# Chunked decay attention and experts on one core: state products in four quarters of the array, state update behind the values, a third first-layer accumulator

## The chip, the cores and the metric

One core of one Trainium2 chip runs the whole program. The metric is device time in microseconds: three runs of the kernel before gave 942.53, 943.29 and 944.0, median 943.29.

## The reference

A decay attention over 4 batches, 8 heads, 768 positions and 48 dimensions per head feeds four experts, each with two layers and a ReLU between them.

```python
for t in range(S):
    cur = einsum('bhd,bhe->bhde', u * k[t], v[t])
    y[:, :, t] = einsum('bhd,bhde->bhe', r[t], state + cur)
    state = w[t][..., None] * state + einsum('bhd,bhe->bhde', k[t], v[t])
x = y.transpose(0, 2, 1, 3).reshape(B * S, H * D)          # 3072 x 384
for e in range(4):
    out += p[:, e:e+1] * (relu(x @ w1[e]) @ w2[e])         # 384 -> 1024 -> 384
```

## The kernel before, in words

The 768 positions are cut into 6 chunks of 128. A chunk of one batch is a **unit**: 24 units, four to a chunk, units 0 to 3 in chunk 0. The 8 heads form 4 pairs. Of a pair i, head j=0 lies on partitions 0 to 47 and head j=1 on 64 to 111 (`half(j)`), so that its products use one half of the rows of the TensorE array; the results of j=0 and j=1 go to the lower and the upper half of the PSUM partitions (`wide(j)`).

A unit goes through six steps, handed out one at a time by `go()`:
- `step_a`: decays of the next unit (DVE), then `scores`: eight products of k and r into two PSUM banks (`sc`, L235), and four transposes of k (`kt`, L241), which ScalarE copies to `ks`.
- `step_b`: the second scan (`e`, L216) and, from chunk 1 on, the decayed state `sd`.
- `step_c`: `masking`, two predicated copies of the scores into `a` (L251).
- `step_d`: scaling of the next unit's r and k, and its diagonal.
- `step_e`: `values`. From chunk 1 on, eight **state products** (`yp`, L261, 48 rows by 48 or 64 columns), then eight **value products** (L266, 128 rows), all in one bank. ScalarE copies the result to `y3` and `x`, VectorE writes the rests that the copies lose (L273 to L276), and `fill` moves the fourth pair by two DMAs into the rows of `x` that are left free.
- `step_f`: `carry`, the **state update**: eight products of 48 moving columns (`up`, L295), which VectorE adds to the state (L300); in chunk 0 ScalarE copies them (L298).

The experts' work is the frame. A turn is one expert on one chunk: eight first-layer tiles of nine products (`f1`, L332; ScalarE writes `hh` at L338 and VectorE `hl` at L339, and only then is the accumulator `pf1` free), then for each batch 24 second-layer products (`f2`, L352). After each f1 tile, and eight times in the second half of a turn, there is a gap; `gap()` adds `pace` to a credit and hands out one step for each whole credit. Chunk 0's first turn is cut into two segments of two batches (256 columns in place of 512), and the second segment needs the x of units 2 and 3. All engines work strictly in the written order. PSUM's eight banks are: two f1 accumulators, two for f2, two for scores (one buffer), two for `kt`, `yp` and `up` in turn.

Of the kernel before, what the change touches and what calls it, by code (L numbers as in the profile page):

```python
# [8 lines left out]
F32 = mybir.dt.float32  # L9
# [11 lines left out]
C = 128  # L21
# [23 lines left out]
def chunked_path(ctx, tc, dmaj, tmaj, u_bc, probs, w1, w2, out, flag):  # L45
    nc = tc.nc

    def pool(name, bufs, space=None):
        kw = {} if space is None else {"space": space}
        return ctx.enter_context(tc.tile_pool(name=name, bufs=bufs, **kw))  # L50
# [7 lines left out]
    p_in = pool("in", 2)  # L58
    p_one = pool("one", 1)
    p_two = pool("two", 2)  # L60
    ps_f1 = pool("ps_f1", 2, PS)
    ps_f2 = pool("ps_f2", 2, PS)
    ps_sc = pool("ps_sc", 1, PS)
    ps_mi = pool("ps_mi", 2, PS)


    ident = const.tile([128, 128], F32, name="ident")
# [161 lines left out]
    def scores(n):  # L229

        s = un[n]
        sc = [ps_sc.tile([128, NP, C], F32, name=f"sc{j}", tag=f"sc{j}") for j in range(2)]
        for i in range(NP):
            for j in range(2):
                nc.tensor.matmul(sc[j][:, i, :], s["kk"][half(j), i, :], s["rr"][half(j), i, :],  # L235
                                 start=True, stop=True)
        last = s["c"] == NCH - 1
        if not last:
            kt = ps_mi.tile([128, NP, 128], F32, name="kt", tag="mi")
            for i in range(NP):  # L240
                nc.tensor.transpose(kt[:, i, 0:ROWS], s["kk"][:, i, :], ident[0:ROWS, 0:ROWS])  # L241
        s["sc"] = sc
        if not last:
            ks = p_one.tile([128, NP, ROWS], F32, name="ks", tag="ks")
            nc.scalar.copy(ks, kt[:, :, 0:ROWS])
            s["ks"] = ks

    def masking(n):
        s = un[n]
        for j in range(2):  # L250
            nc.vector.copy_predicated(s["a"][j], mask.unsqueeze(1).to_broadcast([128, NP, C]), s["sc"][j])  # L251

    def values(n):
        s = un[n]
        c, b, v = s["c"], s["b"], s["v"]
        y = ps_mi.tile([128, NP, C], F32, name="yp", tag="mi")

        if c > 0:
            for i in range(NP):
                for j in range(2):  # L260
                    nc.tensor.matmul(y[wide(j), i, :], sd[n % 2][half(j), i * D:i * D + (64 if j == 0 else D)],  # L261
                                     s["rr"][half(j), i, :], start=(i == 0), stop=False, skip_group_check=True)
        for i in range(NP):
            for j in range(2):
                h = 2 * i + j
                nc.tensor.matmul(y[wide(j), i, :], v[:, h * D:h * D + (64 if j == 0 else D)], s["a"][j][:, i, :],  # L266
                                 start=(c == 0 and i == 0), stop=(i == NP - 1), skip_group_check=True)
        if c not in xb:
            xb[c] = p_x.tile([128, KT, B, 2, C], F32R, name="x", tag="x")
        x = xb[c]  # L270
        y3 = s["y3"] = p_two.tile([ROWS, 2, C], F32R, name="y3", tag="y3")

        nc.scalar.copy(y3[:, 0], y[0:ROWS, KT, :])  # L273
        nc.scalar.copy(x[0:ROWS, :, b, 0, :], y[0:ROWS, 0:KT, :])
        nc.vector.tensor_tensor(y3[:, 1], y[0:ROWS, KT, :], y3[:, 0].bitcast(F32), ALU.subtract)
        nc.vector.tensor_tensor(x[0:ROWS, :, b, 1, :], y[0:ROWS, 0:KT, :], x[0:ROWS, :, b, 0, :].bitcast(F32),  # L276
                                ALU.subtract)

    def fill(n):

        s = un[n]
        for j in range(2):
            nc.sync.dma_start(out=xb[s["c"]][64 * j + D:64 * (j + 1), :, s["b"]].bitcast(F32),
                              in_=s["y3"][half(j)].bitcast(F32))

    def carry(n):
        s = un[n]
        c, b, v = s["c"], s["b"], s["v"]
        if c == NCH - 1:
            return  # L290
        up = ps_mi.tile([128, NP, D], F32, name="up", tag="mi")
        for i in range(NP):
            for j in range(2):
                h = 2 * i + j
                nc.tensor.matmul(up[wide(j), i, :], s["ks"][:, i, wide(j)], v[:, h * D:(h + 1) * D],  # L295
                                 start=True, stop=True)
        if c == 0:
            nc.scalar.copy(st[b], up[0:ROWS])  # L298
        else:
            nc.vector.tensor_tensor(st[b], sd[n % 2][:, 0:NP * D].rearrange("p (i e) -> p i e", i=NP), up[0:ROWS],  # L300
                                    ALU.add)
# [93 lines left out]

    def step_e(n):
        values(n)
        load(n + 2, "r")
        fill(n)
        if n + 1 < NU:  # L400
            guard(n + 1)
        load(n + 3, "w")

    def step_f(n):
        carry(n)
        load(n + 2, "v")
        if n == NU - 1:
            un[n]["big"] = verdict()
        else:
            del un[n]  # L410

    def step_g(n):
        flag_it(un.pop(n)["big"])

    parts = (step_a, step_b, step_c, step_d, step_e, step_f)
    steps = [(f, n) for n in range(NU) for f in parts]
    steps += [(None, NU - 1)] * 8 + [(step_g, NU - 1)]
    steps.reverse()
    read = set()

# [57 lines left out]
    with tc.manual_schedule():  # L478
        act_table()
        setup_a()  # L480
        for what in ("w", "k", "r", "own"):
            load(0, what)
        nc.sync.dma_start(out=u_sb, in_=u_bc)
        load(0, "v")
        warm_up(FILL[0])
        for what in ("w", "k", "r", "own", "v"):
            load(1, what)
        nc.sync.dma_start(out=pr, in_=probs)
        for q in range(NQ):
# [12 lines left out]
        load(2, "own")  # L502
        guard(0)
        load(2, "w")
        own_product(1)
        until_decays(1)
        scale(1)
        warm_up(FILL[1])
        values(0)
        fill(0)  # L510
        own_score(1)
        carry(0)
        load(2, "v")
        scores(1)
        split_w((0, 1, 0), True)
        masking(1)
        after_decays(2)
        own_product(2)
        warm_up(FILL[2])
        values(1)  # L520
        fill(1)
        split_w((0, 1, 1), True)
        guard(1)
        setup_c()
        until_decays(2)
        split_w((0, 1, 2), True)
        carry(1)
        for what in ("w", "k", "r", "v"):
            load(3, what)
        for q in range(3):  # L530
            more_raw()
        scale(2)
        own_score(2)
        load(3, "own")
        split_w((0, 1, 3), True)
        owed.append(None)
        guard(2)
        load(4, "w")
        warm_up(FILL[3])
        del un[0], un[1], steps[-2 * len(parts):]  # L540
        for pi, (g, e) in enumerate(passes):
            first, last = pi % NE == 0, pi % NE == NE - 1
            for blk in g:
                segs = SEG if pi == 0 else (B,)
                b0 = 0
                for nb in segs:
                    next_w1 = blk == g[-1] and pi + 1 in fresh and b0 + nb == B
                    own_w2 = blk == g[0] and pi in fresh and b0 == 0
                    if pi == 0:
                        pace[:] = (0.75, 0.75) if b0 == 0 else (0.25, 0.5)  # L550
                    elif blk >= GROUPS[-1][0]:
                        pace[:] = 0.75, 1.25
                    else:
                        pace[:] = 0.5, 1.0

                    def work(i):
                        q = i % FT // 2
                        if own_w2 and i < FT and i % 2 == 0:
                            split_next((e, 2, q), pi > 0 or q != 1)
                        if next_w1 and i >= FT and i % 2 == 0:  # L560
                            split_next((passes[pi + 1][1], 1, q), True)
                        if i == FT - 1 and last and b0 + nb == B:
                            read.add(blk)

# [193 lines left out]
```

## Time and profile before

| | |
|---|---|
| median of three runs | 943.29 us |
| profiled execution | 942.36 us, span 940.6 us |
| TensorE products busy (PE) | 915.4 us, 97% |
| TensorE weight loads busy (PEld) | 817.9 us, 87% |
| VectorE, ScalarE, GpSimd | 356.2, 254.3, 278.2 us |
| mean granted TensorE clock | 0.985 |

One product in full fp32 shows as two matmul records (x16 for eight products); the fp32r products of the experts show as one. A record's own duration holds the latency of the array, so the time that a group takes is read from the start of the group to the start of the next.

### The profile page before, as it was taken

The page shows a single profiled execution, that of the slowest core. Times are in us where ns is not written, and L with a number is a line of the kernel's source. Part 1 is how long each engine was busy: PE and PEld are TensorE (multiplying, and loading weights), DVE is VectorE, ACT ScalarE, POOL GpSimd, SP SyncE. Part 2 cuts the span into 40 slices and gives each one's busy share as a digit, 9 for nine tenths or more (in the row PEclk, how much of TensorE's full clock was granted, in tenths as well). Part 3 has the DMA queues.
Part 4 walks back from the last instruction along what each step waited for, and adds up shares of the span by engine and source line. Part 5 has one row for each costly group of instructions (what it writes and reads, how often), then busy time and mean ns, then how long its engine had stood idle before and what let it go on. Part 6 is the DMA issues. An engine that isn't in the chain of part 4 may idle for free.

```text
span 940.6 us, 13680 instructions
## 1 busy us (share of the span) xinstructions
PE 915.4 (97%) x5617; PEld 817.9 (87%) x5617; DVE 356.2 (38%) x567; ACT 254.3 (27%) x462; POOL 278.2 (30%) x283
## 2 busy tenths in 40 slices
PE   7589999999999999999999999999999999999997
PEld 5589888898989899889888898998998899899887
DVE  7744545554444532221355553112212212222221
ACT  3434434322224312312321223133103301321210
POOL 4745757431406613304312230024003200131000
PEclk8789999999999999999999999999999999999999
DMA  8544444332215312202322320012001200020001
GB/s 246 179 127 134 132 156 144 120 101 76 87 36 180 107 54 68 68 1 68 102 84 79 100 73 6 22 51 85 1 1 45 74 17 1 1 67 28 16 26 38
DMA packets 34536, 70.49 MB, mean 75 GB/s; under 512 B 4512, under 2 KB 13088, under 8 KB 34464
## 3 DMA queue, kind: packets, MB, share of 16 engines
q1 hardware_dynamic: 34464, 69.52, 23.6%
q8 instruction: 46, 0.75, 0.3%
q14 instruction: 26, 0.21, 0.1%
HBM read 62.43 MB, written 4.72 MB: 71 GB/s over the span
## 4 chain that ended last, share of the span: by engine, by line
PE 95%; DMA 2%; DVE 1%; ACT 1%; issue 0%; SPq 0%
PE pf L352 43%; PE pf L332 42%; PE yp L266 3%; PE sc L235 3%; PE yp L261 2%; PE up L295 1%; PE kt L241 1%; DMA k<-in_dmaj 1%; DMA raw<-in_w 1%; DMA wx<-in_dmaj 0%; DVE w2l L142 0%; DMA x<-y 0%; DVE k L227 0%; ACT w1h L137 0%; ACT wx L307 0%
## 5 line engine op out<-in xcount | busy, mean ns | idle before, releaser
L332 PE MATMUL pf<-x,w1h 128*128 128x512 f32 (+1 forms) x1200 | 364.7, 386 | 12.0 <-DMA x<-y 6.4
L332 PEld LDWEIGHTS pf<-x,w1h 128*128 128x128 f32 x1200 | 223.9, 191 | 55.9 <-issue 7.5
L352 PE MATMUL pf<-w2h,hh 128*128 128x384 f32 x768 | 261.2, 340 | 0.0
L352 PE MATMUL pf<-w2h,hl 128*128 128x384 f32 x768 | 257.1, 335 | 0.0
L352 PE MATMUL pf<-w2l,hh 128*128 128x384 f32 x768 | 256.9, 334 | 0.0
L339 DVE SCALAR_TENSOR_TENSOR hl<-pf,hh 128x512 fp32r<-128x512 f32 (+1 forms) x200 | 133.8, 669 | 280.4 <-ACT hh L338 279.7
L338 ACT ACTIVATE hh<-pf 128x512 fp32r<-128x512 f32 (+1 forms) x200 | 116.2, 581 | 451.1 <-PE pf L332 451.0
L332 PE MATMUL pf<-x,w1l 128*128 128x512 f32 (+1 forms) x600 | 230.5, 384 | 0.0
L142 POOL TENSOR_TENSOR w1l<-raw,w1h 128x384 fp32r<-128x384 f32 x80 | 84.4, 1084 | 255.0 <-ACT w1h L137 254.6
L352 PEld LDWEIGHTS pf<-w2h,hh 128*128 128x128 f32 x768 | 144.2, 188 | 4.8 <-issue 3.3
L352 PEld LDWEIGHTS pf<-w2l,hh 128*128 128x128 f32 x768 | 144.3, 188 | 0.7
L352 PEld LDWEIGHTS pf<-w2h,hl 128*128 128x128 f32 x768 | 144.1, 188 | 0.0
L332 PEld LDWEIGHTS pf<-x,w1l 128*128 128x128 f32 x600 | 114.7, 191 | 21.8
L361 DVE SCALAR_TENSOR_TENSOR acc<-pf,pr,acc 128x384 f32<-128x384 f32 x72 | 44.5, 618 | 201.0 <-PE pf L352 201.0
L142 POOL TENSOR_TENSOR w2l<-raw,w2h 128x384 fp32r<-128x384 f32 x78 | 79.0, 1034 | 115.9 <-ACT w2h L137 110.8
L192 POOL TENSOR_TENSOR a<-ident,dg 128x512 f32<-128x512 f32 x45 | 46.7, 1057 | 133.7 <-DVE dg L184 105.6
L235 PEld LDWEIGHTS sc<-r,k 48*128 48x128 f32 x384 | 24.7, 197 | 12.1 <-DVE k L227 6.1
L235 PE MATMUL sc<-r,k 48*128 48x128 f32 x384 | 29.5, 296 | 5.3 <-DVE k L227 5.3
L204 DVE TENSOR_TENSOR_SCAN g<-wx,ones 112x516 f32<-112x516 f32 x24 | 32.6, 1356 | 3.1 <-DMA wx<-in_dmaj 3.1
L216 DVE TENSOR_TENSOR_SCAN e<-wx,zst 112x516 f32<-112x516 f32 x24 | 33.0, 1373 | 0.8
L177 POOL TENSOR_TENSOR rkt<-rkt 128x384 f32<-128x384 f32 x22 | 28.6, 1299 | 15.6 <-DMA rkt<-in_tmaj 15.6
L137 ACT CAST w2h<-raw 128x768 fp32r<-128x768 f32 x40 | 33.1, 827 | 0.0
(65 smaller groups left out, 438.9 us busy)
## 6 DMA issues: line engine op xcount, KB each, us to landing
raw<-in_w SPq DMA_DIRECT2D x80, 384.0 KB, 3.2
rkt<-in_tmaj SPq DMA_DIRECT2D x23, 384.0 KB, 3.2
wx<-in_dmaj SPq DMA_DIRECT2D x24, 226.2 KB, 3.1
k<-in_dmaj SPq DMA_DIRECT2D x24, 224.0 KB, 2.8
r<-in_dmaj SPq DMA_DIRECT2D x24, 224.0 KB, 3.7
v<-in_tmaj SPq DMA_DIRECT2D x24, 192.0 KB, 2.9
out<-acc SPq DMA_DIRECT2D x24, 192.0 KB, 1.9
x<-y SPq DMA_DIRECT2D x48, 48.0 KB, 2.2
```

Of the source, the lines that this page charges most:

```text
L137: nc.scalar.copy(hi, t)
L142: eng.tensor_tensor(lo[:, s], t[:, s], hi[:, s].bitcast(F32), ALU.subtract)
L177: eng.tensor_tensor(s["rt"], s["rt"], s["kt"], ALU.mult)
L192: nc.gpsimd.tensor_tensor(a, ident.unsqueeze(1).to_broadcast([128, NP, C]), dg[:, q].unsqueeze(2).to_broadcast([128, NP, C]), ALU.mult)
L204: nc.vector.tensor_tensor_scan(g[:, WLEN - 1:0:-1], wx[:, WLEN - 1:0:-1], ones1[:, WLEN - 1:0:-1], 0.0, ALU.mult, ALU.add)
L216: nc.vector.tensor_tensor_scan(e, wx[:, 0:WLEN - 1], zst.rearrange("p i t -> p (i t)"), 0.0, ALU.mult, ALU.add)
L235: nc.tensor.matmul(sc[j][:, i, :], s["kk"][half(j), i, :], s["rr"][half(j), i, :], start=True, stop=True)
L332: nc.tensor.matmul(p[:, 0:nt], wv[:, k, fs], x[:, k, bs, i, :], start=(k == 0 and n == 0), stop=(k == KT - 1 and n == 2))
L338: nc.scalar.activation(hh[:, ts], p[:, 0:nt], AF.Relu)
L339: nc.vector.scalar_tensor_tensor(hl[:, ts], p[:, 0:nt], 0.0, hh[:, ts].bitcast(F32), ALU.max, ALU.subtract)
L352: nc.tensor.matmul(p, hv[:, ts], wv[:, o, :], start=(f == 0 and n == 0), stop=(f == FT - 1 and n == 2))
L361: nc.vector.scalar_tensor_tensor(a[:, b, :], p, sc, a[:, b, :], ALU.mult, ALU.add)
```

## The change

1. The state products of pairs 1 and 3 go to the other half of the columns (`o = j ^ (i % 2)`), and to a second bank. Pairs 0 and 2 keep theirs. So of four state products in a row, each has its own quarter of the array (row half by column half).
2. `yp` therefore has two banks and is taken from the scores' buffer (`tag="sc"`). From chunk 1 on, pairs 0 and 2 go by ScalarE and VectorE into `x` (two tiles), pairs 1 and 3, which stand with their heads swapped, into `y3`; `fill` has four DMAs in place of two and puts the heads in their places.
3. `carry` stands directly behind `values` in one step; there are five steps to a unit, and `pace` is lowered to about five sixths.
4. One bank goes from `ps_mi` to the f1 accumulators: three of these, and one buffer for `kt` and `up`.

```diff
-    ps_f1 = pool("ps_f1", 2, PS)
+    ps_f1 = pool("ps_f1", 3, PS)
-    ps_mi = pool("ps_mi", 2, PS)
+    ps_mi = pool("ps_mi", 1, PS)
...
-        sc = [ps_sc.tile([128, NP, C], F32, name=f"sc{j}", tag=f"sc{j}") for j in range(2)]
+        sc = ps_sc.tile([128, 2, NP, C], F32, name="sc", tag="sc")
...
-        y = ps_mi.tile([128, NP, C], F32, name="yp", tag="mi")
+        yp = ps_sc.tile([128, 2, NP, C], F32, name="yp", tag="sc")
+        if c == 0:
+            y = yp.rearrange("p g (i z) t -> p (g i) z t", z=2)[:, :, 0, :]
+        else:
+            y = [yp[:, i % 2, i // 2, :] for i in range(NP)]
             for i in range(NP):
                 for j in range(2):
-                    nc.tensor.matmul(y[wide(j), i, :], sd[n % 2][half(j), i * D:i * D + (64 if j == 0 else D)],
-                                     s["rr"][half(j), i, :], start=(i == 0), stop=False, skip_group_check=True)
+                    o = j ^ (i % 2)
+                    nc.tensor.matmul(y[i][wide(o)], sd[n % 2][half(j), i * D:i * D + (64 if o == 0 else D)],
+                                     s["rr"][half(j), i, :], start=(i < 2), stop=False, skip_group_check=True)
...
+        for dst, src in places(s, y if c == 0 else yp):
+            nc.scalar.copy(dst[:, :, 0], src)
+        for dst, src in places(s, y if c == 0 else yp):
+            nc.vector.tensor_tensor(dst[:, :, 1], src, dst[:, :, 0].bitcast(F32), ALU.subtract)
...
+            if s["c"] > 0:
+                nc.sync.dma_start(out=x[half(j), 1, s["b"]].bitcast(F32), in_=y3[half(o), 0].bitcast(F32))
...
     def step_e(n):
         values(n)
+        carry(n)
         load(n + 2, "r")
         fill(n)
...
-                        pace[:] = (0.75, 0.75) if b0 == 0 else (0.25, 0.5)
+                        pace[:] = (0.625, 0.625) if b0 == 0 else (0.2, 0.4)
...
-                        pace[:] = 0.5, 1.0
+                        pace[:] = 0.4, 0.8
```

How the order of work moves, at three places. First TensorE at unit 4, the first with a state; `yp` are the values, `up` the state update, `pf` the experts' products. Before:

```order
L266 MATMUL yp<-a_687,v 48x128
L352 MATMUL pf_914<-w2h,hh 128x384
L352 MATMUL pf_914<-w2l,hh 128x384
L352 MATMUL pf_914<-w2h,hl 128x384
L352 MATMUL pf_914<-w2h,hh 128x384
```

Now:

```order
L277 MATMUL yp<-a_687,v 48x128
L277 MATMUL yp<-a_689,v 48x128
L315 MATMUL up<-v,ks 64x48
L315 MATMUL up<-v,ks 48x48
L315 MATMUL up<-v,ks 64x48
```

The twelve expert products that stood between the values and the state update are gone from there.

Second, VectorE in the first segment, from the third f1 tile's `hl` on; `w2l` is a weight split, `zst` and `e` belong to step b of unit 2, `a` is the masking of unit 2. Before:

```order
L339 SCALAR_TENSOR_TENSOR hl<-pf_456,hh 128x256
L142 TENSOR_TENSOR w2l<-raw,w2h 128x384 x2
L214 TENSOR_SCALAR zst<-g 112x4
L215 RECIPROCAL zst<-zst 112x4
L216 SCALAR_TENSOR_TENSOR e<-wx,zst 112x516
L339 SCALAR_TENSOR_TENSOR hl<-pf_481,hh 128x256
L251 COPY_PREDICATED a_375<-mask,sc_435 128x512
L251 COPY_PREDICATED a_377<-mask,sc_436 128x512
L339 SCALAR_TENSOR_TENSOR hl<-pf_497,hh 128x256
```

Now:

```order
L359 SCALAR_TENSOR_TENSOR hl<-pf_453,hh 128x256
L142 TENSOR_TENSOR w2l<-raw,w2h 128x384 x2
L359 SCALAR_TENSOR_TENSOR hl<-pf_474,hh 128x256
L214 TENSOR_SCALAR zst<-g 112x4
L215 RECIPROCAL zst<-zst 112x4
L216 SCALAR_TENSOR_TENSOR e<-wx,zst 112x516
L359 SCALAR_TENSOR_TENSOR hl<-pf_492,hh 128x256
L251 COPY_PREDICATED a_373<-mask,sc 128x512
L251 COPY_PREDICATED a_375<-mask,sc 128x512
```

The fourth `hl` moved ahead of step b's scan, the fifth ahead of the masking.

Third, ScalarE at the end of the first segment; `acc` is the end of a batch's second layer, `y` and `x` the copies of unit 3's values, `hh` the first f1 tile of the second segment. Before:

```order
L359 ACTIVATE acc<-pf_612,pr 128x384
L273 CAST y_706<-yp 112x128
L274 CAST x<-yp 112x3x128
L306 ACTIVATE wx<-wx,mid 112x4x128
L307 ACTIVATE wx,chk<-wx,edge 112x4x128
L359 ACTIVATE acc<-pf_668,pr 128x384
L298 COPY st_108<-up 112x192
L338 ACTIVATE hh<-pf_738 128x256
```

Now:

```order
L379 ACTIVATE acc<-pf_609,pr 128x384
L379 ACTIVATE acc<-pf_662,pr 128x384
L285 CAST y_709<-yp 112x128
L285 CAST x<-yp 112x2x128
L318 COPY st_108<-up 112x192
L326 ACTIVATE wx<-wx,mid 112x4x128
L327 ACTIVATE wx,chk<-wx,edge 112x4x128
L358 ACTIVATE hh<-pf_734 128x256
```

Unit 3's values moved behind the last second-layer products of the segment.

## Rows read from the trace of the kernel before

**Rows 1.** The page's first lines: span, busy time and share of engines.
```profile
span 940.6 us, 13680 instructions
PE 915.4 (97%) x5617; PEld 817.9 (87%) x5617; DVE 356.2 (38%) x567; ACT 254.3 (27%) x462; POOL 278.2 (30%) x283
```

**Rows 2.** The chain that ended last, by line.
```profile
PE pf L352 43%; PE pf L332 42%; PE yp L266 3%; PE sc L235 3%; PE yp L261 2%; PE up L295 1%; PE kt L241 1%; DMA k<-in_dmaj 1%; DMA raw<-in_w 1%; DMA wx<-in_dmaj 0%; DVE w2l L142 0%; DMA x<-y 0%; DVE k L227 0%; ACT w1h L137 0%; ACT wx L307 0%
```

**Rows 3.** TensorE's waits: total us, times, longest us.
```profile
PE pf L332 <- DMA x<-y: 6.4, 2, 3.7
PE pf L332 <- DVE hl L339: 5.6, 3, 3.7
```

**Rows 4.** Timeline, values of unit 15: start us, us, engine, line, count.
```profile
321.99 0.34 PE L352 MATMUL pf<-w2h,hl 128*128 128x384 f32 x1
322.25 0.84 PEld L261 LDWEIGHTS yp<-r,sd 48*64 48x64 f32 x16 [0.25 <-issue]
322.25 1.08 PE L261 MATMUL yp<-r,sd 48*64 48x128 f32 x16
323.27 1.09 PE L266 MATMUL yp<-a,v 128*64 128x128 f32 x16
324.29 0.45 PE L352 MATMUL pf<-w2h,hh 128*128 128x384 f32 x1
324.57 0.34 PE L352 MATMUL pf<-w2l,hh 128*128 128x384 f32 x1
```

**Rows 5.** Timeline at two instants, 322.60 and 323.04: L261 products then in flight.
```profile
322.41 0.39 PE L261 MATMUL yp<-r,sd 48*48 48x128 f32 x4
...
322.84 0.39 PE L261 MATMUL yp<-r,sd 48*48 48x128 f32 x4
```

**Rows 6.** Timeline, state update of unit 15.
```profile
326.31 0.34 PE L352 MATMUL pf<-w2h,hl 128*128 128x384 f32 x1
...
326.57 0.67 PE L295 MATMUL up<-v,ks 128*64 128x48 f32 x16
...
327.45 0.34 PE L352 MATMUL pf<-w2l,hh 128*128 128x384 f32 x1
```

**Rows 7.** Timeline, unit 1: its state update directly behind its values.
```profile
22.03 0.28 PE L266 MATMUL yp<-a,v 128*48 128x128 f32 x1
22.05 0.61 PE L295 MATMUL up<-v,ks 128*64 128x48 f32 x14
...
22.60 1.20 PE L108 MATMUL pf<-zero 128*128 128x512 f32 x4
```

**Rows 8.** Timeline, scores and transposes of unit 16.
```profile
329.45 1.16 PE L235 MATMUL sc<-r,k 48*128 48x128 f32 x16
...
330.55 0.61 PE L241 MATMUL kt<-ident,k 112*128 112x112 f32 x4
```

**Rows 9.** Timeline, what empties the values of unit 15.
```profile
324.44 0.27 ACT L273 CAST y<-yp 112x128 fp32r<-112x128 f32 x1 [3.58 <-PE yp L266]
...
325.32 0.55 DVE L276 TENSOR_TENSOR x<-yp,x 112x384 fp32r<-112x384 f32 x1
```

**Rows 10.** Timeline, TensorE at the ends of waits in the first turn.
```profile
44.59 0.51 PE L332 MATMUL pf<-x,w1h 128*128 128x256 f32 x2 [3.67 <-DVE hl L339]
...
51.70 0.44 PE L352 MATMUL pf<-w2h,hh 128*128 128x384 f32 x1
...
66.55 0.77 PE L332 MATMUL pf<-x,w1h 128*128 128x256 f32 x2 [2.77 <-DMA x<-y]
```

**Rows 11.** Timeline, VectorE in the first segment.
```profile
39.62 2.38 DVE L142 TENSOR_TENSOR w2l<-raw,w2h 128x384 fp32r<-128x384 f32 x2 [0.30 <-ACT w2h L137]
...
42.33 1.89 DVE L216 TENSOR_TENSOR_SCAN e<-wx,zst 112x516 f32<-112x516 f32 x1
44.14 0.39 DVE L339 SCALAR_TENSOR_TENSOR hl<-pf,hh 128x256 fp32r<-128x256 f32 x1
44.45 1.34 DVE L251 COPY_PREDICATED a<-mask,sc 128x512 f32<-128x512 uint32 x2
```

More of the change, by code (lines that the diff above doesn't have):

```diff
@@ L231, in scores @@
         s = un[n]
-        sc = [ps_sc.tile([128, NP, C], F32, name=f"sc{j}", tag=f"sc{j}") for j in range(2)]
+        sc = ps_sc.tile([128, 2, NP, C], F32, name="sc", tag="sc")
         for i in range(NP):
             for j in range(2):
-                nc.tensor.matmul(sc[j][:, i, :], s["kk"][half(j), i, :], s["rr"][half(j), i, :],
+                nc.tensor.matmul(sc[:, j, i, :], s["kk"][half(j), i, :], s["rr"][half(j), i, :],
                                  start=True, stop=True)
@@ L250, in masking @@
         for j in range(2):
-            nc.vector.copy_predicated(s["a"][j], mask.unsqueeze(1).to_broadcast([128, NP, C]), s["sc"][j])
+            nc.vector.copy_predicated(s["a"][j], mask.unsqueeze(1).to_broadcast([128, NP, C]), s["sc"][:, j])
     def values(n):
@@ L255, in values @@
         c, b, v = s["c"], s["b"], s["v"]
-        y = ps_mi.tile([128, NP, C], F32, name="yp", tag="mi")
-        if c > 0:
+        yp = ps_sc.tile([128, 2, NP, C], F32, name="yp", tag="sc")
[3 more added lines that the diff above has]
+            y = [yp[:, i % 2, i // 2, :] for i in range(NP)]
             for i in range(NP):
                 for j in range(2):
-                    nc.tensor.matmul(y[wide(j), i, :], sd[n % 2][half(j), i * D:i * D + (64 if j == 0 else D)],
-                                     s["rr"][half(j), i, :], start=(i == 0), stop=False, skip_group_check=True)
+                    o = j ^ (i % 2)
+                    nc.tensor.matmul(y[i][wide(o)], sd[n % 2][half(j), i * D:i * D + (64 if o == 0 else D)],
+                                     s["rr"][half(j), i, :], start=(i < 2), stop=False, skip_group_check=True)
         for i in range(NP):
@@ L265, in values @@
                 h = 2 * i + j
-                nc.tensor.matmul(y[wide(j), i, :], v[:, h * D:h * D + (64 if j == 0 else D)], s["a"][j][:, i, :],
-                                 start=(c == 0 and i == 0), stop=(i == NP - 1), skip_group_check=True)
+                if c == 0:
+                    nc.tensor.matmul(y[wide(j), i, :], v[:, h * D:h * D + (64 if j == 0 else D)],
+                                     s["a"][j][:, i, :], start=(i % 2 == 0), stop=(i % 2 == 1),
+                                     skip_group_check=True)
+                else:
+                    nc.tensor.matmul(y[i][half(j ^ (i % 2))], v[:, h * D:(h + 1) * D], s["a"][j][:, i, :],
+                                     start=False, stop=(i >= 2), skip_group_check=True)
         if c not in xb:
@@ L270, in values, with places @@
         x = xb[c]
[L271 to L277, printed above, removed]
+        y3 = s["y3"] = p_two.tile([ROWS, 2, 2, C], F32R, name="y3", tag="y3")
+        for dst, src in places(s, y if c == 0 else yp):
+            nc.scalar.copy(dst[:, :, 0], src)
+        for dst, src in places(s, y if c == 0 else yp):
+            nc.vector.tensor_tensor(dst[:, :, 1], src, dst[:, :, 0].bitcast(F32), ALU.subtract)
+    def places(s, y):
+        x, y3 = xb[s["c"]][0:ROWS, :, s["b"]], s["y3"]
+        if s["c"] == 0:
+            return (y3[:, 1:2], y[0:ROWS, 3:4]), (x, y[0:ROWS, 0:3])
+        return (y3, y[0:ROWS, 1, 0:2]), (x[:, 0::2], y[0:ROWS, 0, 0:2])
     def fill(n):
         s = un[n]
+        x, y3 = xb[s["c"]], s["y3"]
         for j in range(2):
-            nc.sync.dma_start(out=xb[s["c"]][64 * j + D:64 * (j + 1), :, s["b"]].bitcast(F32),
-                              in_=s["y3"][half(j)].bitcast(F32))
+            o = 1 - j if s["c"] > 0 else j
+            nc.sync.dma_start(out=x[64 * j + D:64 * (j + 1), :, s["b"]].bitcast(F32),
+                              in_=y3[half(o), 1].bitcast(F32))
+            if s["c"] > 0:
+                nc.sync.dma_start(out=x[half(j), 1, s["b"]].bitcast(F32), in_=y3[half(o), 0].bitcast(F32))
     def carry(n):
@@ L402, in step_e @@
         load(n + 3, "w")
-    def step_f(n):
-        carry(n)
         load(n + 2, "v")
@@ L410, in step_f @@
             del un[n]
-    def step_g(n):
+    def step_f(n):
         flag_it(un.pop(n)["big"])
-    parts = (step_a, step_b, step_c, step_d, step_e, step_f)
+    parts = (step_a, step_b, step_c, step_d, step_e)
     steps = [(f, n) for n in range(NU) for f in parts]
-    steps += [(None, NU - 1)] * 8 + [(step_g, NU - 1)]
+    steps += [(None, NU - 1)] * 8 + [(step_f, NU - 1)]
     steps.reverse()
@@ L509, in chunked_path @@
         values(0)
+        carry(0)
         fill(0)
         own_score(1)
-        carry(0)
         load(2, "v")
@@ L520, in chunked_path @@
         values(1)
+        carry(1)
         fill(1)
@@ L526, in chunked_path @@
         split_w((0, 1, 2), True)
-        carry(1)
         for what in ("w", "k", "r", "v"):
@@ L549, in chunked_path @@
                     if pi == 0:
-                        pace[:] = (0.75, 0.75) if b0 == 0 else (0.25, 0.5)
+                        pace[:] = (0.625, 0.625) if b0 == 0 else (0.2, 0.4)
                     elif blk >= GROUPS[-1][0]:
-                        pace[:] = 0.75, 1.25
+                        pace[:] = 0.6, 1.0
                     else:
-                        pace[:] = 0.5, 1.0
+                        pace[:] = 0.4, 0.8
                     def work(i):
```

## The prediction

> **What bounds the kernel now.** I read the page's first lines, then the chain that ended last, then TensorE's waits, then the timeline of one unit in mid-run and of the first turn. The reader is to see in the first that TensorE's products are busy for 97% of the span and no other engine for half of it [rows 1]; in the chain, that the experts' two layers make up 85% and the attention's small products the next ten or so, with the state products (L261) at 2%, the state update (L295) at 1% [rows 2]. The experts' products wait 12 us in all, in five places, on x from the DMAs or on `hl` [rows 3], and both kinds lie in the first turn [rows 10]. So in mid-run a microsecond of TensorE taken away is a microsecond of time, as long as nothing new makes TensorE wait; in the first turn the waits decide.
>
> The sum is made against the profiled execution, 942.36 us, which is 0.93 below the median 943.29; I add 0.93 at the end.
>
> **State products in four quarters.** Unit 15 stands for all 20 units with a state (4 to 23). Its state products start at 322.25 and the value products at 323.27: 1.02 us for 16 passes of eight products [rows 4]. At two instants four passes are in flight, two just started and two before them; the older ones started at 322.41 and at 322.84, which lie four steps of one pair apart [rows 5]: 0.43 / 4 = 0.108 us a step, 8 steps for 16 passes. With four passes to a step it would be 4 steps, and 0.43 us a unit goes, 20 x 0.43 = 8.6 us. The weights' first load and the change of shape at both ends (1.02 less 0.86) stay.
>
> No row shows four at once, so bounds are needed. The scores run the two row halves against the same columns into two banks: 16 passes between 329.45 and 330.55, 0.069 us each, under the 0.108 that one takes, so two at a time [rows 8]. The value products use all rows and two column halves: 16 passes in 1.02 us again [rows 4]. Each direction of the split thus runs at once, also with 128 moving columns of fp32, and the change has each row half write its own bank where columns are shared. Weight loads would come every 0.43 / 16 = 0.027 us; the state update's 16 loads and 16 passes took 0.67 us with the latency of the last in it [rows 6], not far from that rate. The ends are 8.6 and 0; I take 8.6, since both nearest rows show full overlap. The end below nothing is the fourth rival.
>
> **State update behind the values.** Now it is a block by itself: from the expert product before it at 326.31 to the second one behind it at 327.45 [rows 6] is 1.14 us, in which two regular steps also lie. A regular step is (326.31 - 324.57) / 10 = 0.174 us, ten products apart [rows 4, 6]. So a block costs 1.14 - 0.35 = 0.79 us. What it costs directly behind the values is seen at unit 1: from its last value product at 22.03 to the next other product at 22.60 is 0.57 us [rows 7]. Without the update that distance is 0.21: the last value pass of unit 15 started at 323.27 + 1.09 - 0.28 = 324.08 (0.28 is one pass's own length [rows 7]) and the next product came at 324.29 [rows 4]. That makes 0.36 at the least, because in unit 1 one column half had begun early, and 0.57 at the most; I take 0.44, nearer the first. The saving is 0.35 a unit, with ends 0.22 and 0.43. It counts for units 4 to 19: 16 x 0.35 = 5.6 us (3.5 to 6.9). Units 0 to 3 lie in the opening, units 20 to 23 update no state.
>
> **Values in the scores' banks.** This adds a wait: the next unit's scores cannot start before both ScalarE copies and both VectorE subtractions have read the values. Now they end at 325.32 + 0.55 = 325.87 [rows 9], 1.79 us after the last value product. The new copies have 256 + 256 columns for 128 + 384, the same total. In the order of the changed kernel at least twelve second-layer or nine first-layer products stand between, 12 x 0.174 = 2.09, and before them the update's 0.44 and the 0.21: about 2.7 us, 0.9 more than needed; in the last chunk, without update, 0.5 more. I price it at nothing. The cover is that those products keep TensorE busy. Queued behind a waiting score product on TensorE are the transposes and all expert products; VectorE's next scaling and masking wait for them.
>
> **One buffer for `kt` and `up`.** The transposes now wait for the state addition, directly behind the subtractions; they come 1.10 us after the scores' start [rows 8], so 3.8 us after the values against some 2.2 for the addition. Nothing.
>
> **Two more DMAs a unit.** SP issues four fills where it issued two, and the loads of w and v two units on queue behind them. The x of a chunk with a state is first read, by the order, at least 72 second-layer products (12.5 us) after its last unit's values. Nothing; without that cover each of five chunks would show a wait like the 2.77 us of the first turn [rows 10].
>
> **The opening: third accumulator, step order, E of unit 3.** In the first segment TensorE waits for `hl` three times, 5.6 us [rows 3]. The third accumulator lets each f1 tile go one `hl` earlier. VectorE then sets the pace: its weight split ends at 39.62 + 2.38 = 42.0; the fourth `hl` (0.39) now follows at once, 42.4, where it ended at 44.5; then the two small steps of 0.33 and the scan of 1.89, to 44.6, the fifth `hl` to 45.0 and the masking of 1.34 to 46.3 [rows 11]. The eighth f1 tile starts at 45.0 in place of the sixth at 44.59 [rows 10] and is done when the masking is. Values of unit 2 take 1.02 and the update 0.44: the second layer starts at about 48.0 against 51.70 [rows 10], 3.7 us earlier. But unit 3's values now stand behind the segment's last six second-layer products, 6 x 0.174 = 1.04 us later in the order, and the second segment's first tile waits for their x through copies, subtraction and DMA. So its start at 66.55 [rows 10] comes 2.7 us earlier, and the wait before it grows from 2.77 to about 4.2. I take 2.7. Ends: 3.7 saved, if the later place costs nothing; 1.0 lost, if VectorE or GpSimd are late again and only the later place remains.
>
> **A rule against it.** In the trace 16 weight loads lie inside the state products' block, 0.84 us of load time in its 1.02 [rows 4], so a load runs beside a pass in the same row half. The Trainium skill says otherwise (TensorE: Matmul & The Clock Gate, Part 3: Packing small matmuls, The mechanism): a weight load overlaps running products only when its row group differs. By that rule two quarters that share rows would take turns in loading, and the four-quarter form would lose; rival four has its time from rows.
>
> **Sum.** 8.6 + 5.6 + 2.7 = 16.9; 942.36 - 16.9 = 925.5, and with 0.93, 926.4 us.
>
> **Rivals.**
> *Quarters in one row half or column half do not run together.* For it: no row has four. Against it: rows 4 and 8. Then 8.6 stays: 935.0 us.
> *The opening gives nothing.* For it: VectorE's chain there has splits, scans and masking in one queue, and unit 3's values come later. Against it: the moved `hl`. 926.4 + 2.7 = 929.1, or with 1.0 lost, 930.1 us.
> *The scores wait for the emptied values, and the kernel is slower.* Place: each unit's first score product, 22 of them in the turns. A decay scan of 1.89 [rows 11] ahead of the subtractions on VectorE would move their end from 1.8 to 3.7 us, 1.0 past the 2.7 there are: 22 us more, 948.4 us. It decides from 16.9 / 22 = 0.8 us a unit, that is with subtractions ending 3.5 us after the values. Against it: at unit 15 ScalarE had been idle for 3.58 us when the values came [rows 9].
> *Loads and passes of quarters that share rows take turns.* Per row half 8 passes of 0.108 plus a load of about 0.05 (0.84 / 16 [rows 4]) make 1.28 us in place of 0.86: 0.42 x 20 = 8.4 lost and not 8.6 gained, 943.4 us, no change. Against it: the loads inside the block.
>
> **How the numbers follow.** Forecast 0.72 (its own range 922.5 to 931), quarters 0.11, opening 0.09, scores wait 0.05, turns 0.03. About 0.2% (1.9 us) is what a measurement of this kernel can tell from no change. Faster: 0.72 + 0.11 + 0.09 = 0.92, of which I move 0.01 to what I have not thought of; same 0.04; slower 0.05. The range goes from 921.5, where the opening and the update save their most, to 935.5, which takes in the first rival.
>
> **What would show it.** Right: the state products' group lasts 0.6 us from its start to the value products' start, not 1.02; the state update follows the values with no gap and the next expert product comes 0.55 to 0.65 us after the last value product; TensorE's waits name no `sc <- DVE` on the values; the segment's second layer starts near 48 and the second segment near 64 us. Wrong: state products still at 1.0 us, a wait of the scores on the subtractions in each unit, or a second segment that starts at 66 us or later.

## The result: 13.5 us faster, where 16.9 were forecast

The changed kernel takes 929.44 us (median of 4 runs, 928.05 to 930.68), the kernel before 942.93 in the same comparison (4 runs, 942.53 to 944.0): a ratio of 0.9855, interval 0.9838 to 0.9872. That is 13.5 us less by the medians, where 16.9 were forecast. The profiled executions differ by 14.3 us, 928.05 against 942.36; the one of the changed kernel happens to be the lowest of its four. What follows is worked out between these two, by their spans: 926.3 against 940.6.

The page's first lines, to be laid beside [rows 1] and [rows 2] (the lines of the experts' products are L352 and L372 now, the state products L267, the values L273 and L277, the state update L315):

```profile
span 926.3 us, 13725 instructions
PE 901.4 (97%) x5617; PEld 811.2 (88%) x5617; DVE 359.6 (39%) x567; ACT 254.7 (27%) x462; POOL 279.1 (30%) x283
...
PE pf L372 44%; PE pf L352 42%; PE sc L235 3%; PE yp L277 2%; PE yp L267 1%; PE kt L241 1%; PE up L315 1%; DMA k<-in_dmaj 1%; DMA raw<-in_w 1%; PE yp L273 0%; DVE w2l L142 0%; DMA x<-y 0%; DVE k L227 0%; DVE e L216 0%; PE pf L108 0%
```

TensorE issues as many products as before (5617), is busy for 14 us less, and still for 97% of the span. In the chain the state products have gone from 2% to 1%.

The timeline of one unit in mid-run (start us, us, engine, line, operation, count), against [rows 4], [rows 6] and [rows 9]:

```profile
320.07 0.34 PE L372 MATMUL pf<-w2h,hl 128*128 128x384 f32 x1
320.33 0.43 PEld L267 LDWEIGHTS yp<-r,sd 48*64 48x64 f32 x16 [0.25 <-issue]
320.33 0.67 PE L267 MATMUL yp<-r,sd 48*64 48x128 f32 x16
...
320.93 1.08 PE L277 MATMUL yp<-a,v 128*48 128x128 f32 x16
...
321.84 0.61 PE L315 MATMUL up<-v,ks 128*64 128x48 f32 x16
322.09 0.37 ACT L285 CAST y<-yp 112x256 fp32r<-112x256 f32 x1 [11.54 <-PE yp L277]
...
322.39 0.44 PE L372 MATMUL pf<-w2h,hh 128*128 128x384 f32 x1
322.67 0.34 PE L372 MATMUL pf<-w2l,hh 128*128 128x384 f32 x1
...
323.11 0.41 DVE L287 TENSOR_TENSOR x<-yp,x 112x256 fp32r<-112x256 f32 x1
...
323.91 0.33 PE L372 MATMUL pf<-w2h,hl 128*128 128x384 f32 x1
```

The state products last 0.60 us until the values start (before 1.02). The update stands right behind the values. The last value pass started at 320.93 + 1.08 - 0.28 = 321.73 and the next expert product at 322.39, 0.66 later (forecast 0.55 to 0.65). The subtractions end at 323.52, 1.79 after that pass, as before; no score product has to wait for them here, and the chunk's four DMAs hold up nothing. At an instant in the block, 320.75, the timeline has more passes in flight than the four of [rows 5] (by the page's records, whose ends are modelled):

```profile
320.49 0.51 PE L267 MATMUL yp<-r,sd 48*48 48x128 f32 x12
```

TensorE's waits, beside [rows 3]:

```profile
PE pf L352 <- DMA x<-y: 7.0, 2, 4.2
PE sc L235 <- DVE k L227: 4.2, 2, 2.3
PE pf L352 <- DVE hl L359: 2.5, 2, 1.6
PE sc L235 <- DVE x L287: 2.0, 1, 2.0
```

The waits for `hl` fell from 5.6 to 2.5 us. The wait of scores on values, which by the prediction was not to be named at all, exists, but once: unit 1's scores, in the prologue, at 17.57 us. There is none in the turns.

The timeline of TensorE in the opening, beside [rows 10]:

```profile
44.94 0.51 PE L352 MATMUL pf<-x,w1h 128*128 128x256 f32 x2 [1.56 <-DVE hl L359]
...
47.16 0.61 PE L315 MATMUL up<-v,ks 128*64 128x48 f32 x16
47.70 0.44 PE L372 MATMUL pf<-w2h,hh 128*128 128x384 f32 x1
...
63.69 0.77 PE L352 MATMUL pf<-x,w1h 128*128 128x256 f32 x2 [4.16 <-DMA x<-y]
```

The second layer starts at 47.70 (forecast 48.0, before 51.70), the second segment at 63.69 (forecast 63.85, before 66.55) after a wait of 4.16 (forecast 4.2). So far the steps came out as written. What was left out comes right behind it. Two stretches of before, then of after (length; busy us and count of PE, PEld, DVE, ACT, POOL; then the granted clock as a share of 2.4 GHz, DMA share and GB/s):

```profile
60.00:65.00 5.00, 3.78 (x44) 2.98 (x42) 0.76 (x2) 2.76 (x7) 3.04 (x4) 1.00 0.47 139
65.00:70.00 5.00, 3.45 (x17) 3.48 (x18) 0.42 (x1) 0.38 (x1) 0.98 (x1) 0.66 0.34 97
```

```profile
60.00:65.00 5.00, 1.31 (x6) 1.35 (x7) 0.56 (x2) 1.42 (x3) 1.99 (x2) 0.77 0.44 131
65.00:70.00 5.00, 5.00 (x27) 5.00 (x27) 0.85 (x2) 1.00 (x3) 0.00 (x0) 0.55 0.00 0
```

With the longer wait the granted clock of this execution is at its lower level (1.2 GHz) for longer: in the trace's clock records from 62.7 us for 6.8 us, before from 66.4 for 3.4. The first 24 products of the second segment take 5.26 us, before 4.38. At the 217th product of the experts, the first of the segment's last batch and so a mark behind the opening, the lead of 2.86 is down to 1.96. Before, then after:

```profile
82.72 0.33 PE L352 MATMUL pf<-w2h,hh 128*128 128x384 f32 x1
```

```profile
80.76 0.33 PE L372 MATMUL pf<-w2h,hh 128*128 128x384 f32 x1
```

The end of the program, the last expert product and what follows it, before and after:

```profile
934.16 0.34 PE L352 MATMUL pf<-w2h,hl 128*128 128x384 f32 x1
...
934.54 0.62 DVE L361 SCALAR_TENSOR_TENSOR acc<-pf,pr,acc 128x384 f32<-128x384 f32 x1 [3.55 <-PE pf L352]
935.19 0.33 SPq L364 DMA_DIRECT2D out<-acc  x1
```

```profile
918.37 0.34 PE L372 MATMUL pf<-w2h,hl 128*128 128x384 f32 x1
...
918.74 0.62 DVE L381 SCALAR_TENSOR_TENSOR acc<-pf,pr,acc 128x384 f32<-128x384 f32 x1 [3.55 <-PE pf L372]
919.39 0.33 SPq L384 DMA_DIRECT2D out<-acc  x1
```

The addition and the output's DMA follow at the same distance, yet the span ends 926.3 - 918.4 = 7.96 us behind the last product, and 940.6 - 934.2 = 6.48 before (from the records before rounding).

**Where the 14.3 us are.** From the starts of TensorE's products I took, for each block of small products, the time by which it sets back the experts' products around it: from the start of the one before it to the start of the ninth behind it, less nine regular steps of 0.1736 us. For unit 15 that is 323.91 - 320.07 - 1.56 = 2.28.

| | before | after | saved |
|---|---|---|---|
| block of state, values and update (16 units) | 2.237 + 0.797 | 2.278 | 0.756 x 16 = 12.1 |
| block of state and values (4 units) | 2.237 | 1.811 | 0.426 x 4 = 1.7 |
| start of the experts' 217th product | 82.72 | 80.76 | 1.96 (lead at the segment's start 2.86) |
| last product to end of span | 6.48 | 7.96 | -1.48 |

The sum is 14.3, the whole difference. The prediction counted a block only to the second product behind it; that way the new block is 2.253 (unit 15: 322.67 - 320.07 - 0.35 = 2.25). But with the update in it the fourth and the sixth product behind it come late too, 0.185 and 0.182 us after the one before them in place of 0.174: 0.025 us a unit, 0.4 in all. The blocks of before don't have that, nor do the four without an update.

### The profile page after: what moved, and what is told of

It reads as the page before. It is cut to its first block, busy times and chain, and to the rows that moved or that the text cites. A ratio compares the mean times of both kernels' runs of the same rounds, so it can differ in the third digit from the quotient of the medians.

```text
span 926.3 us, 13725 instructions
## 1 busy us (share of the span) xinstructions
PE 901.4 (97%) x5617; PEld 811.2 (88%) x5617; DVE 359.6 (39%) x567; ACT 254.7 (27%) x462; POOL 279.1 (30%) x283
## 4 chain that ended last, share of the span: by engine, by line
PE 94%; DVE 2%; DMA 2%; ACT 1%; issue 1%; SPq 0%; DVEq 0%
PE pf L372 44%; PE pf L352 42%; PE sc L235 3%; PE yp L277 2%; PE yp L267 1%; PE kt L241 1%; PE up L315 1%; DMA k<-in_dmaj 1%; DMA raw<-in_w 1%; PE yp L273 0%; DVE w2l L142 0%; DMA x<-y 0%; DVE k L227 0%; DVE e L216 0%; PE pf L108 0%
## 5 line engine op out<-in xcount | busy, mean ns | idle before, releaser
L352 PE MATMUL pf<-x,w1h 128*128 128x512 f32 (+1 forms) x1200 | 365.0, 387 | 9.5 <-DMA x<-y 7.0
L352 PEld LDWEIGHTS pf<-x,w1h 128*128 128x128 f32 x1200 | 224.6, 192 | 52.5 <-issue 4.4
L372 PE MATMUL pf<-w2h,hh 128*128 128x384 f32 x768 | 259.3, 338 | 0.0
L372 PE MATMUL pf<-w2h,hl 128*128 128x384 f32 x768 | 257.1, 335 | 0.0
L372 PE MATMUL pf<-w2l,hh 128*128 128x384 f32 x768 | 256.8, 334 | 0.0
L352 PE MATMUL pf<-x,w1l 128*128 128x512 f32 (+1 forms) x600 | 231.2, 385 | 0.0
L372 PEld LDWEIGHTS pf<-w2h,hh 128*128 128x128 f32 x768 | 144.2, 188 | 2.2 <-issue 0.6
L372 PEld LDWEIGHTS pf<-w2l,hh 128*128 128x128 f32 x768 | 144.2, 188 | 0.8
L372 PEld LDWEIGHTS pf<-w2h,hl 128*128 128x128 f32 x768 | 144.2, 188 | 0.0
L352 PEld LDWEIGHTS pf<-x,w1l 128*128 128x128 f32 x600 | 115.1, 192 | 21.8
L142 POOL TENSOR_TENSOR w2l<-raw,w2h 128x384 fp32r<-128x384 f32 x78 | 82.6, 1080 | 106.7 <-ACT w2h L137 100.8
L251 DVE COPY_PREDICATED a<-mask,sc 128x512 f32<-128x512 uint32 x48 | 32.1, 723 | 3.4 <-POOL a L192 2.1
L379 ACT ACTIVATE acc<-pf,pr 128x384 f32<-128x384 f32 x24 | 14.0, 582 | 70.3 <-PE pf L372 70.2
```

The costliest lines, as they stand in the source:

```text
L142: eng.tensor_tensor(lo[:, s], t[:, s], hi[:, s].bitcast(F32), ALU.subtract)
L352: nc.tensor.matmul(p[:, 0:nt], wv[:, k, fs], x[:, k, bs, i, :], start=(k == 0 and n == 0), stop=(k == KT - 1 and n == 2))
L372: nc.tensor.matmul(p, hv[:, ts], wv[:, o, :], start=(f == 0 and n == 0), stop=(f == FT - 1 and n == 2))
```

## The experiments

Theory: the four quarters give 0.43 us a unit, the update 0.35, the third accumulator brings the opening forward; the longer wait then costs clock, and the program's end 1.5 us. The rivals: the quarters give nothing and another part does it; the accumulator moves a wait only; the longer end is chance. Intervals are those of the ratio to the kernel before, which was measured beside each of three groups of experiments (medians 942.79, 942.37 and 942.57 us).

**Two quarters.** The changed kernel with the array split as before:

```
-                    o = j ^ (i % 2)
+                    o = j
...
-                    nc.tensor.matmul(y[i][half(j ^ (i % 2))], v[:, h * D:(h + 1) * D], s["a"][j][:, i, :],
+                    nc.tensor.matmul(y[i][half(j)], v[:, h * D:(h + 1) * D], s["a"][j][:, i, :],
...
-            o = 1 - j if s["c"] > 0 else j
+            o = j
```

> The changed kernel with pairs 1 and 3 put back on their own column half: the state products use two quarters of the array again, everything else (two banks, four fills, update behind the values, three accumulators) stays. Theory, four quarters run at once: the state products' group goes back to 1.0 us, 0.43 us a unit and 20 units make 8.5 us more, about 938.0 against the changed kernel's 929.4. Rival, the gain came with the second bank and not with the quarters: 929.4.

Measured: 936.73 us (935.79 to 937.26), 0.9933 [0.992, 0.9947]. Its timeline in mid-run:

```profile
325.07 1.08 PE L267 MATMUL yp<-r,sd 48*64 48x128 f32 x16
326.08 1.08 PE L277 MATMUL yp<-a,v 128*48 128x128 f32 x16
327.00 0.61 PE L315 MATMUL up<-v,ks 128*64 128x48 f32 x16
327.54 0.45 PE L372 MATMUL pf<-w2h,hh 128*128 128x384 f32 x1
```

The state products are back at 1.01 us; the rest of the block is as in the changed kernel. The block costs 2.698 against 2.278: 0.42 us a unit, 8.4 for 20; the spans differ by 8.5, the medians by 7.3. The quarters are a term of their own and of the forecast size.

**The update alone.** The kernel before with the state update directly behind the values:

```
     def step_e(n):
         values(n)
+        carry(n)
...
     def step_f(n):
-        carry(n)
```

> The kernel before with nothing changed but the state update moved directly behind the values; six steps, their pace, two accumulators and two quarters stay. Theory, the update gets cheaper because it joins a group of the same shape: a block of 0.80 us becomes 0.44 to 0.45 more in the values' group, 16 units make 5.7 us, about 937.3 against 942.9. Rival, it costs the same wherever it stands: 942.9.

Measured: 937.58 us (936.4 to 938.38), 0.994 [0.9926, 0.9954]; 5.2 us by the medians.

```profile
321.07 0.62 PE L295 MATMUL up<-v,ks 128*48 128x48 f32 x16
321.62 0.45 PE L352 MATMUL pf<-w2h,hh 128*128 128x384 f32 x1
```

To the second product behind it, the block costs 2.686 in place of 2.237 + 0.797 = 3.034: 0.348 us a unit, 5.6 for 16. To the ninth it costs 2.711, so 0.323 a unit and 5.2 for 16, which is what the medians show. Its end is 6.51 us, that of before; it issues two fills a unit, like before.

**Two accumulators.** The changed kernel with the buffers as before:

```
-    ps_f1 = pool("ps_f1", 3, PS)
+    ps_f1 = pool("ps_f1", 2, PS)
...
-    ps_mi = pool("ps_mi", 1, PS)
+    ps_mi = pool("ps_mi", 2, PS)
```

> The changed kernel with two first-layer accumulators and two buffers for transposes and update, as before. Theory, the third accumulator only matters in the opening, where each tile waits one hl longer: the second layer of the first segment starts 1.6 us later (49.3 in place of 47.7), total 1 to 2 us more, about 931, mid-run unchanged. Rival A, the reordered hl alone made the opening faster: 929.4. Rival B, the third accumulator made all 4.0 us of it: 933.

Measured: 929.92 us (928.21 to 931.11), 0.9856 [0.9841, 0.9871], only 0.5 above the changed kernel.

```profile
45.74 0.54 PE L352 MATMUL pf<-x,w1h 128*128 128x256 f32 x2 [1.86 <-DVE hl L359]
66.95 0.77 PE L352 MATMUL pf<-x,w1h 128*128 128x256 f32 x2 [4.18 <-DMA x<-y]
```

The first segment's second layer starts at 51.06, 3.4 us later than in the changed kernel (1.6 were expected), and the second segment 3.3 us later, yet the median is nearly the same. It settles nothing by itself: its spell at the lower clock is 3.4 us and not 6.8, its first 24 products take 4.28, and runs of one kernel spread by as much as the difference sought. So the clock had to be taken out of the comparison.

**The clock held.** The changed kernel with 14 products on zeros ahead of the second segment, in the wait:

```
+                    if pi == 0 and b0 > 0:
+                        warm_up(14)
```

> The changed kernel with 14 products on zeros in the wait of 4.2 us before the second segment (they add nothing to the result). In the changed kernel the granted clock is half for two stretches around that wait, 62.7 to 69.5, where the kernel before had one. Theory, the longer idle of TensorE costs the clock and so eats part of the opening's gain: with the products the first-layer tiles from 63.7 on take 0.36 us for three products and not 0.64, and the total falls by 1.3 to 2.9 us, to about 927. Rival, the wait and not the clock is what is lost: 929.4, or later if the products delay the first tile.

Measured: 926.91 us (924.97 to 929.26), 0.9832 [0.9812, 0.9852]. The same two stretches as above:

```profile
60.00:65.00 5.00, 4.48 (x42) 3.51 (x38) 0.76 (x2) 2.54 (x7) 3.12 (x4) 1.00 0.58 158
65.00:70.00 5.00, 4.76 (x40) 4.79 (x41) 1.27 (x3) 1.32 (x4) 0.05 (x1) 1.00 0.22 77
```

The granted clock stays at its higher level, 40 products fit where 27 did, and the first 24 of the segment take 2.95 us in place of 5.26. The segment had started 1.6 us later in this execution (65.24; its first expert product had come 1.95 later), and its 217th product still comes 1.0 us earlier, at 79.75. By the medians 2.5 us come back, though the two intervals overlap: two of its five runs took 929.1 and 929.3 at a mean granted clock of 0.984, the other three 925.0 to 926.9 at 0.989 to 0.991. Without a trace of those two, where they lost clock is not known.

**Two accumulators with the clock held.** Both edits above together.

> The changed kernel with two first-layer accumulators (and two buffers for transposes and update) and the 14 products on zeros that gave 926.91 with three. With two the second segment started at 66.95 and not at 63.68 in the profiles, but the totals differed by only 0.5. Theory, the clock hid the third accumulator's worth: with the clock held in both, two accumulators take 2 to 3 us more, about 929.5. Rival, the third accumulator is worth nothing in time: 926.9.

Measured: 929.6 us (927.75 to 932.06), 0.9864 [0.9844, 0.9884]; the 217th product starts at 81.64. The start of the first segment's second layer with three accumulators (the run above), then with two:

```profile
49.31 0.44 PE L372 MATMUL pf<-w2h,hh 128*128 128x384 f32 x1
```

```profile
50.92 0.44 PE L372 MATMUL pf<-w2h,hh 128*128 128x384 f32 x1
```

The first expert product stands at 29.16 in both. Against the run with three (217th product at 79.75, median 926.91) the third accumulator is worth 1.6 us here, 1.9 at the 217th product and 2.7 by the medians, whose intervals just overlap. So the gain is there when the clock doesn't cover it. It is not all of the 4.0 us by which the second layer starts earlier after the change; the rest would be the new order's, which was not tried alone.

**Unit 3's values six products earlier.** In the changed kernel one number of the table that sets the order:

```
-                        pace[:] = (0.625, 0.625) if b0 == 0 else (0.2, 0.4)
+                        pace[:] = (0.625, 0.75) if b0 == 0 else (0.2, 0.4)
```

> The changed kernel with the pace of the first segment's second layer at 0.75 in place of 0.625, so that the values of unit 3 stand six second-layer products earlier again and the scores of unit 4 behind those products, in the wait for x. Theory, the later place of unit 3's values cost 1.04 us and the scores in the wait are free: the second segment starts 1.0 us earlier and 1.65 us of scores leave the segment, 1 to 2.7 us less, about 927.5. Rival, VectorE is late with the masking when it has one gap less, and nothing is gained: 929.4.

Measured: 925.74 us (924.28 to 926.18), 0.9823 [0.9809, 0.9836]; 3.7 us under the changed kernel, 2.0 under its repeat in the same comparison (below).

```profile
45.82 0.79 PE L352 MATMUL pf<-x,w1h 128*128 128x256 f32 x2 [1.56 <-DVE hl L359]
65.99 0.48 PE L352 MATMUL pf<-x,w1h 128*128 128x256 f32 x2 [1.14 <-DMA x<-y]
```

The wait for x is 1.14 us, and the first 24 products of the segment take 2.94: most of the changed kernel's wait comes from the place at which its order puts unit 3's values, as the prediction said, and with real work in it (unit 4's scores stand there now) the clock does not fall. The segment does not start 1.0 us earlier, as expected, but 2.3 later: in this execution the first expert product came 1.6 later, and a spell at the lower clock lay in the first segment, from 45.1 to 51.9. The 217th product, with unit 4's scores now ahead of the segment, still comes at 78.86, 1.9 us earlier.

**Empty instructions on SyncE.** 40 of them in the setup of the changed kernel:

```
+        for i in range(40):
+            nc.sync.nop(nofuse=True)
```

> The changed kernel with 40 empty instructions in SyncE's program ahead of the first turn; nothing else. From the last TensorE product to the end of the span the changed kernel took 7.95 us and the one before 6.48; the two kernels with four fills that ran so far took 7.8 to 8.1, the one with two fills 6.5. Theory, the 40 fill DMAs made SyncE's program longer so that an instruction fetch falls into its last semaphores, 1.25 us: 40 more instructions move the fetch out of there, the end takes 6.5 us again and the total falls by 1.4, to 928.0. Rival, the longer end comes from the DMAs themselves or from the last output: it stays at 7.9, 929.4.

Measured: 927.75 us (925.41 to 931.4), 0.9849 [0.9826, 0.9872], an end of 7.85. None of the 40 is in the trace, so it tells nothing of the end. It is a second measurement of the changed kernel: its nine runs lie between 925.4 (mean granted clock 0.988) and 931.4 (0.980). In its profile the first expert product comes 1.55 us later than in the first one's, which is more than the 1.4 by which the two executions differ.

**Three edits.** Unit 3's values earlier, 6 products on zeros ahead of the second segment, and the same empty instructions.

> The changed kernel with the pace of 0.75, 6 products on zeros in the rest of the wait (they add nothing to the result) and the 40 empty instructions on SyncE. If the three add up: 929.4 less 1.4 less 2.0 less 1.5, about 924.5. If clock and place are the same loss counted twice: about 926.5.

Measured: 924.08 us (923.18 to 925.14), 0.9809 [0.9796, 0.9823]; the end is 7.87. The first two edits give 3.7 us against the repeat in the same comparison (5.4 against the first measurement); the third did nothing. That the time is near the 924.5 expected is luck: 1.4 of that sum was for the end, which stayed.

**A longer program on SyncE.** The changed kernel with 32 loads of one number each, in the middle of the run, where nothing waits for them:

```
+        for i in range(32):
+            nc.sync.dma_start(out=pad[0:1, i:i + 1], in_=probs[0:1, 0, 0:1])
```

> The changed kernel with 32 loads of one number each on SyncE's queue at about 580 us, where that queue is quiet; nobody reads them. The 40 empty instructions of e5 did not reach the chip's program (SyncE's records are 576 as in the changed kernel, and the gap of 1.2 us stands at the same place among its last semaphores), so the question of the end is open. Theory, an instruction fetch falls there because of the program's length: it moves away, the last product to the end takes 6.5 us and not 7.9, the total falls by 1.4 in the profile. Rival, it has to do with the fills themselves or the outputs: 7.9 stays.

Measured: 926.96 us (925.44 to 927.27), 0.9833 [0.9815, 0.9852]; 2.5 us under the changed kernel, while the profiles differ by 1.1, since its opening was 0.4 slower. The transfers of instructions on queue q14 by the page, before, after and here:

```profile
q14 instruction: 26, 0.21, 0.1%
```

```profile
q14 instruction: 27, 0.22, 0.1%
```

```profile
q14 instruction: 26, 0.21, 0.1%
```

And this run's last lines (lines of code are one higher here):

```profile
918.78 0.34 PE L373 MATMUL pf<-w2h,hl 128*128 128x384 f32 x1
919.16 0.62 DVE L382 SCALAR_TENSOR_TENSOR acc<-pf,pr,acc 128x384 f32<-128x384 f32 x1 [3.55 <-PE pf L373]
919.80 0.33 SPq L385 DMA_DIRECT2D out<-acc  x1
```

The span is 925.2: 6.45 us behind the last product, as before the change. In the changed kernel's records SyncE's final semaphore instructions have a gap of 1.25 us, from 924.05 to 925.30. Behind the last output's DMA q14 has five transfers of 8192 bytes, the fourth at 923.71, just ahead of the gap, and the fifth at 925.96, behind it. With the 32 loads the gap is gone, and there are four such transfers. So it is in all twelve profiles: five transfers and 7.75 to 8.07 us from the last product to the end in the eight kernels with four fills and no loads, four and 6.45 to 6.67 in the other four. So the longer end is not chance. (The page's count alone does not tell: it is 27 for the update alone too, where one of them is of 72 bytes, at the start.) More work on SyncE made the end shorter, which excludes the number of its instructions by itself; that it matters where a block of them ends is the reading that fits. The Trainium skill (Runtime: NRT & Kernel Launch, Instruction fetch mechanics) says that an engine's instructions are fetched in blocks while it executes earlier ones. If the gap is such a fetch, it is not hidden in the last microseconds here.

**All that helped.** Unit 3's values earlier, 6 products on zeros ahead of the second segment, and the 32 loads.

> The kernel of e7 (unit 3 earlier, 6 products on zeros in the rest of the wait; its empty instructions taken out) with the same 32 small loads. If the end shortens as the theory has it: 924.1 less 1.4, about 922.7. If not: 924.1.

Measured: 922.84 us (921.93 to 924.3), 0.9794 [0.9775, 0.9813].

```profile
62.09 1.64 PE L109 MATMUL pf<-zero 128*128 128x512 f32 x6
64.02 0.48 PE L353 MATMUL pf<-x,w1h 128*128 128x256 f32 x2 [0.29 <-DMA x<-y]
```

The wait of 4.16 is down to 0.29, the end to 6.67. It is the fastest of all, 6.6 us under the changed kernel and 20 under the one before.

## Why the forecast was right, and where it was too high

- **State products.** Forecast 0.43 us a unit, 8.6 in all. Measured 0.426 (4 units without an update) and, against the run with two quarters, 0.42. The choice of the full end was right: the two directions of the split, each read from other products, hold together too. The rule that was weighed is of the Trainium skill (TensorE: Matmul & The Clock Gate, Part 3: Packing small matmuls, The mechanism): a weight load overlaps running products only when its row group differs. The trace has 16 weight loads inside the block's 0.60 us, with two quarters in each row half, so it doesn't hold for these quarters. Rival four, where loads and passes take turns, had 1.28 us for the passes, which with the 0.16 of both ends makes a block of 1.44.
- **Update.** Forecast 0.35 a unit, measured 0.348 alone when counted as in the prediction, to the second product behind. The 0.025 in the products behind that was not looked at, so 0.32 is left, and 0.4 us of the sum are missing.
- **Scores on the values, one buffer for `kt` and `up`.** Nothing in the turns, as forecast. The prologue's 2.0 us were not seen ahead. In this execution the first expert product still comes 0.26 us earlier than before (27.21 against 27.47), which is luck in part: in the nine other profiles with the values in the scores' banks it comes at 27.39 to 30.27, in five of them at 28.8 or later, for the update alone at 28.05. How much of that is the wait and how much the DMAs and the clock of the prologue, no run separates.
- **Opening: right in mechanism, too large.** All its times were met within about 0.4 us. The step that failed is "I take 2.7": it carried the gain at the segment's start unchanged through the segment. TensorE's clock falls in that wait, and in this execution for longer than before. The first 24 products cost 2.31 us more than at the full clock (5.26 less 2.95), where before the change it was already 1.43 (4.38 less 2.95); 2.86 of lead became 1.96. How much is lost differs by execution. The wait is 4.16 in four profiles with this opening: in two (the changed kernel and its repeat) the 24 products take 5.26, in two others (two quarters, the 32 loads) 4.43 and 4.24, hardly more than before the change or less. So the run that holds the clock shows that the clock takes time there; that the longer wait cost more of it than the shorter one had is so only in the first two, and 0.74 us, what the step was too large by, is the size for this profile.
- **A term left out: the end.** "Two more DMAs a unit. Nothing" was right about queues and waits. It did not look at the program of SyncE, which issues them and whose final semaphores now have the gap of 1.25 us. The run with the longer program shows that this goes away; that the blocks' boundary is what decides is the reading that fits, not shown for other lengths.
- **Profile and median.** 16.9 less 0.4 (update), 0.74 (opening) and 1.48 (end) is 14.3, the difference of the profiles. The median gave 0.8 less: the profiled execution was the fastest of four, and in the profiles of these runs the prologue's length and the opening's spells at the lower clock differ each time.

Of the rivals' times one was met, and by chance: 929.1 to 930.1 us was the forecast for an opening that gives nothing. It gave 1.96 us in the profile, and the third accumulator alone 1.6 to 1.9 with the clock held, so that the number fits and the reason does not; the end and the other terms above make up the difference. The others were missed. The one on the slower side, the scores that wait in each unit, had its wait in none of its 22 places, and once ahead of them.

## What to carry to other kernels

Where TensorE sets the time, idle quarters of the array and small blocks that stand alone are time that can be counted from the trace before: a pair of nearest rows, one for each direction of the split, gave the size to 0.01 us. Such a block is counted until the products behind it keep their regular step again. An edit that makes TensorE arrive earlier at a wait that stays does not carry its whole lead past it: look at the granted clock behind that wait, and fill the wait with work that is needed anyway (here the next unit's scores). Look at the distance from the last product to the end too: an edit that adds to a queue's program can move it.

## What was not expected of the hardware

- The passes of four quarters run together, loads included: 16 passes in 0.60 us (two quarters: 1.01), 12 in flight at an instant by the records.
- A wait of 4.16 us went with 6.8 us at the lower clock in two profiles and with 3.4 in two others, one of 2.77 with 3.4: the length of the wait alone doesn't set it. With products on zeros in the wait it did not fall.
- A gap of 1.25 us in the program's last semaphores, beside a fifth transfer of 8192 bytes of instructions, went away with 32 more DMA instructions.
- Empty instructions given to SyncE did not reach the program: 576 records with and without them.
